# A two-stage mixture kernel: an in-place weight conversion with a leaky activation, a new plan for block 1's tokens and a reciprocal's correction factor in PSUM

## The chip, the cores and the metric

The kernel runs on one core of one Trainium2 chip. The metric is the time of one execution on the device in microseconds (us), the median of three runs. A core has TensorE (matmuls, PE in the rows; its weight loads are PEld), VectorE (DVE), ScalarE (ACT), GpSimd (POOL) and SyncE, whose queue (SP) issues all the DMAs here. Each engine works through its own instructions in order and waits on semaphores for the others.

## The reference

Attention with pooled keys and values, then two dense layers with a nonlinearity between, then a gated pair of them:

```python
k_p = k.reshape(B, H, Sp, 8, D).mean(axis=3)          # v_p likewise; B=8, H=8, S=576, D=64
scores = q @ k_p.T / sqrt(D)
x = softmax(scores) @ v_p                             # 4608 tokens x 512

h = x @ w_in                                          # 512 -> 2048
P = a[0] + a[1]*h + a[2]*h**2 + a[3]*h**3
Q = 1.0 + abs(b[0])*abs(h) + abs(b[1])*h**2
x = (P / (Q + 1e-6)) @ w_out                          # 2048 -> 512

gate = 1.0 / (1.0 + exp(-(x @ w_gate)))               # 512 -> 1536
out = (gate * (x @ w_val)) @ w_out2                   # 1536 -> 512
```

q, k, v are float32, the weights float64. The result has float32 accuracy, so each matmul operand is held as a high and a low part (hi and lo), and each product takes three matmuls (lines 485 to 487).

## The kernel before

**First stage.** The 4608 tokens are nine blocks of 512. For each block the hidden layer is walked in 16 steps of 128 columns, 144 steps n in all, `f = n % 16`. Step n multiplies block `n // 16` by weight slice f (`g1`, 12 matmuls, output h in PSUM), makes the rational function of h (`rational1` to `rational3`), splits the previous step's result into hi and lo (`split_g`) and multiplies step n - 3's result by its slice of w_out (`g2`, 12 matmuls, accumulated over the block in four banks acc). Four other PSUM banks rotate for everything else: h, and the scores, transposes and outputs of attention (sc, pta and ptb, psx).

**The rational function.** ScalarE makes s = h², u = |b0 h| and a linear y from h, VectorE makes u = Q - 1 and y towards P (lines 528 to 530). ScalarE writes a guess of 1/Q over h in PSUM, by way of Ln and Exp (`rational2`, line 538). `rational3` makes one correction step on VectorE: line 542 forms u = (u + 1) times the guess, line 543 y = P times the guess, line 544 y = (u - 2) times y. The bank of h comes free once its last reader is done, line 543.

**Attention beside it.** A block's tokens lie in four or five tiles (`token_tiles`). Tile i has a step `at[i]`; scores go on TensorE three steps ahead of it, exponential and normalisation (line 388 on GpSimd) two steps ahead. For tiles with `at[i] > NF1` ("late") the transposes stand in step `at[i]` behind g1 and the attention matmuls (`attend`, psx) in the step after, behind g1; for the others the transposes end step `at[i] - 1`, and `attend` stands in step `at[i]`. Block 1's five tiles have steps 3, 5, 7, 10, 12. `attend` writes xs, the block's input of g1. `on_pe` parts 0 and 1 of a step stand behind g1 and behind g2; `off_pe` parts 0, 1 and 2 hold the other engines' work. Keys and values of the next batch are pooled and masked by the same plan (`pool_k`, `pool_v`, `mask_v`).

**Weights.** They come as float64. A word pair is turned into a float32 pair in place: `conv1a` scales the high word's float view and the low word on ScalarE; `conv1b`, run by `gap()` between `rational2` and `rational3` of the next step, shifts the high word left by three into a work tile wx, puts its sign bit back by AND and OR (both VectorE), and adds the low word (GpSimd). `conv2` makes hi (ScalarE) and lo (GpSimd, line 118). In block 0 `weights_a` brings one slice of w_in and one of w_out through this per step: conv2 of w_in's slice n + 3 and w_out's n, conv1 of n + 5 and n + 2. From step 16 on `background` prepares the twelve units of the second stage's weights, eight steps each, 96 steps in all, and writes them to DRAM.

**Second stage.** From the end of step 143 on (`gate`, `value`, `h2`), it works on 768 tokens at a time in six rounds. The change doesn't touch it.

Line 542 to 544, in full:

```python
nc.vector.scalar_tensor_tensor(out=u, in0=u, scalar=ONE, in1=r, op0=ALU.add, op1=ALU.mult)
nc.vector.scalar_tensor_tensor(out=y, in0=y, scalar=coef[:, 0:1], in1=r, op0=ALU.add, op1=ALU.mult)
nc.vector.scalar_tensor_tensor(out=y, in0=u, scalar=-2.0, in1=y, op0=ALU.add, op1=ALU.mult)
```

## Time and profile before

| what | us |
|---|---|
| timed runs, median (lowest to highest) | 1896.74 (1896.67 to 1898.65) |
| profiled execution | 1894.58 |
| its span, first to last instruction | 1892.7 |
| prologue, to the first activation of step 0 | 44.6 |
| block 0 (steps 0 to 15) | 157.9 |
| blocks 1 to 6 | 657.3 |
| block 7 | 100.2 |
| block 8 and the second stage | 932.7 |

A block is counted from the first activation on its first h (line 525) to that of the next block. Busy time of an engine is the time in which it had an instruction under way; a TensorE that is busy all the time need not be at its peak, since each matmul's end is modelled. PEclk is the granted share of TensorE's full clock. A wait row says who waited, for whom, how long in total, how often, and the longest. A line number is that of kernel.py before.

### The profile page before, as it was taken

How to read it: one execution, taken by the hardware profiler on the slowest of the kernel's cores; microseconds unless marked ns; L12 is line 12 of the kernel's file. 1: busy time of each engine (PE TensorE's matmuls, PEld its weight loads, DVE VectorE, ACT ScalarE, POOL GpSimd, SP SyncE). 2: the span in 40 equal slices, each digit the busy share in tenths (PEclk: the TensorE clock that was granted, in tenths of full speed). 3: DMA queues.
4: the chain of work that ended last, by engine and by line, in shares of the span. 5: the costliest groups of instructions: out<-in, count | busy, mean ns of one | idle time of the engine just before them, and what ended most of it. 6: DMA issues, size and time to landing. Idle time of an engine off the chain costs nothing.

```text
span 1892.7 us, 25138 instructions
## 1 busy us (share of the span) xinstructions
PE 1804.6 (95%) x8936; PEld 1564.4 (83%) x8936; DVE 1242.5 (66%) x1847; ACT 943.0 (50%) x1754; POOL 896.4 (47%) x855
## 2 busy tenths in 40 slices
PE   5578999999999999999999999999999999999999
PEld 4467788787777788788887999998998998998997
DVE  7999999999998899988778543343334333333331
ACT  4777777677676777776666422222222222222221
POOL 6768556565564665653224234334235225235231
PEclk9799999999999999999999999999999999999999
DMA  7343355343544553443154574574573664663661
GB/s 247 131 153 120 107 191 187 135 171 135 186 159 156 192 176 137 168 148 119 56 196 150 190 236 153 166 235 133 184 228 123 211 211 129 222 201 112 206 203 43
DMA packets 123117, 312.56 MB, mean 165 GB/s; under 512 B 11504, under 2 KB 43248, under 8 KB 122992
## 3 DMA queue, kind: packets, MB, share of 16 engines
q1 hardware_dynamic: 122992, 310.95, 48.7%
q8 instruction: 71, 1.16, 0.2%
q14 instruction: 54, 0.44, 0.1%
HBM read 257.95 MB, written 52.95 MB: 164 GB/s over the span
## 4 chain that ended last, share of the span: by engine, by line
PE 67%; DVE 21%; ACT 4%; issue 4%; DMA 2%; POOL 2%; SPq 0%; ACTq 0%; POOLq 0%; DVEq 0%
PE h L485 13%; PE h L487 12%; PE h L486 12%; PE acc L485 3%; PE acc L487 3%; PE acc L486 3%; PE accA L722 3%; PE accA L723 3%; PE h L722 3%; PE h L723 3%; PE accA L721 3%; PE h L721 3%; DVE u L528 3%; PE psx L413 3%; DVE y L544 3%
## 5 line engine op out<-in xcount | busy, mean ns | idle before, releaser
L658 DVE TENSOR_TENSOR t<-h,t 128x384 f32<-128x384 f32 x360 | 200.7, 557 | 387.0 <-ACT t L666 276.2
L513 POOL TENSOR_TENSOR g<-y,g 128x512 fp32r<-128x512 f32 x144 | 190.6, 1324 | 245.7 <-ACT g L510 186.7
L711 POOL TENSOR_TENSOR t<-t 128x384 f32<-128x384 f32 x72 | 84.4, 1172 | 448.9 <-issue 253.7
L485 PE MATMUL h<-xs,wi 128*128 128x512 f32 x576 | 234.4, 407 | 11.8 <-DVE xs L420 5.2
L485 PE MATMUL acc<-g,wo 128*128 128x512 f32 x576 | 232.8, 404 | 2.2 <-ACT g L510 2.2
L487 PE MATMUL h<-xs,wi 128*128 128x512 f32 x576 | 229.3, 398 | 3.0 <-DVE xs L420 3.0
L486 PE MATMUL h<-xs,wi 128*128 128x512 f32 x576 | 229.2, 398 | 0.0
L487 PE MATMUL acc<-g,wo 128*128 128x512 f32 x576 | 226.0, 392 | 2.4 <-POOL g L513 2.4
L486 PE MATMUL acc<-g,wo 128*128 128x512 f32 x576 | 225.0, 391 | 0.0
L487 PE MATMUL h<-xS,wq 128*128 128x384 f32 x576 | 193.1, 335 | 0.0
L485 PE MATMUL h<-xS,wq 128*128 128x384 f32 x576 | 192.9, 335 | 0.0
L486 PE MATMUL h<-xS,wq 128*128 128x384 f32 x576 | 192.7, 335 | 0.0
L528 DVE SCALAR_TENSOR_TENSOR u<-s,coef,u 128x512 f32<-128x512 f32 x144 | 132.1, 918 | 32.2 <-ACT u L526 31.9
L485 PE MATMUL h<-xA,wq 128*128 128x384 f32 x432 | 149.0, 345 | 0.0
L544 DVE SCALAR_TENSOR_TENSOR y<-u,y 128x512 f32<-128x512 f32 x144 | 143.9, 999 | 4.9
L487 PE MATMUL h<-xA,wq 128*128 128x384 f32 x432 | 144.7, 335 | 0.0
L486 PE MATMUL h<-xA,wq 128*128 128x384 f32 x432 | 144.6, 335 | 0.0
L485 PEld LDWEIGHTS h<-xs,wi 128*128 128x128 f32 x576 | 111.3, 193 | 39.1 <-DVE xs L420 4.2
L525 ACT ACTIVATE s<-h 128x512 f32<-128x512 f32 x144 | 85.0, 590 | 110.4 <-PE h L487 110.3
L542 DVE SCALAR_TENSOR_TENSOR u<-u,h 128x512 f32<-128x512 f32 x144 | 98.5, 684 | 56.0 <-ACT h L538 54.3
L487 PEld LDWEIGHTS h<-xs,wi 128*128 128x128 f32 x576 | 111.1, 193 | 27.9 <-DVE xs L420 3.5
L485 PEld LDWEIGHTS acc<-g,wo 128*128 128x128 f32 x576 | 108.5, 188 | 27.9 <-ACT g L510 2.6
(122 smaller groups left out, 4300.2 us busy)
## 6 DMA issues: line engine op xcount, KB each, us to landing
wq<-w2d SPq DMA_DIRECT2D x252, 512.0 KB, 4.3
wo<-wod SPq DMA_DIRECT2D x88, 512.0 KB, 3.8
w2d<-wq SPq DMA_DIRECT2D x36, 512.0 KB, 2.9
x2d<-o SPq DMA_DIRECT2D x36, 256.0 KB, 2.4
out_dram<-o SPq DMA_DIRECT2D x36, 256.0 KB, 2.0
raw<-in_k_dram SPq DMA_DIRECT2D x32, 256.0 KB, 2.8
raw<-in_q_dram SPq DMA_DIRECT2D x32, 256.0 KB, 2.7
raw<-in_v_dram SPq DMA_DIRECT2D x32, 256.0 KB, 3.1
```

The source lines that it names most:

```text
L485: nc.tensor.matmul(out_, wl, xh, start=start, stop=False, skip_group_check=on)
L486: nc.tensor.matmul(out_, wh, xh, start=False, stop=False, skip_group_check=on)
L487: nc.tensor.matmul(out_, wh, xl, start=False, stop=stop, skip_group_check=on)
L513: eng.tensor_tensor(out=g[:, 1], in0=y, in1=g[:, 0].bitcast(F32), op=ALU.subtract)
L525: nc.scalar.activation(s, h, AF.Square)
L528: nc.vector.scalar_tensor_tensor(out=u, in0=s, scalar=coef[:, 5:6], in1=u, op0=ALU.mult, op1=ALU.add)
L542: nc.vector.scalar_tensor_tensor(out=u, in0=u, scalar=ONE, in1=r, op0=ALU.add, op1=ALU.mult)
L544: nc.vector.scalar_tensor_tensor(out=y, in0=u, scalar=-2.0, in1=y, op0=ALU.add, op1=ALU.mult)
L658: nc.vector.tensor_tensor(out=out_, in0=a, in1=b, op=ALU.add)
L721: nc.tensor.matmul(a[t], gh, wt[:, 0], start=(f == 0), stop=False)
L722: nc.tensor.matmul(a[t], gh, wt[:, 1], start=False, stop=False)
L723: nc.tensor.matmul(a[t], gl, wt[:, 0], start=False, stop=(f == NF2 - 1))
```

## The change

Six edits. In the conversion the Copy on the high word becomes a Prelu with the slope 2^32 on negative values: positive values are scaled by 2^-112 and negative ones by 2^-80, and the bits of the exponent in which these differ are such that the shift by three puts the sign bit where it belongs. The AND/OR instruction and the work tile wx go, and the shift writes in place. lo of w_in's slices is made on VectorE. Background's twelve units are spread over 112 steps (9 or 10 each, the last ones idle). Block 1's tiles get steps 2, 5, 8, 11, 14 and the late order (`late_` for every `at[i] > 0`), and pooled values and masks follow. `rational3` takes y first, writes the correction factor over the guess in PSUM, and multiplies from there. Of a block's four stores three and not two are copied by ScalarE.

```diff
-            nc.scalar.activation(hw.bitcast(F32), hw.bitcast(F32), AF.Copy, scale=2.0 ** -112)
+            nc.scalar.activation(hw.bitcast(F32), hw.bitcast(F32), AF.Prelu, scale=2.0 ** -112, alpha=2.0 ** 32)
...
-        ws = [(raw[:, :, 1], raw[:, :, 0], new_tmp("wx").bitcast(I32)[:, :raw.shape[1]]) for raw in raws]
-        for hw, lw, x in ws:
-            nc.vector.tensor_scalar(out=x, in0=hw, scalar1=3, scalar2=None, op0=ALU.logical_shift_left)
-        for hw, lw, x in ws:
-            nc.vector.scalar_tensor_tensor(out=hw, in0=hw, scalar=-2 ** 31, in1=x, op0=ALU.bitwise_and, op1=ALU.bitwise_or)
-        for hw, lw, x in ws:
+        ws = [(raw[:, :, 1], raw[:, :, 0]) for raw in raws]
+        for hw, lw in ws:
+            nc.vector.tensor_scalar(out=hw, in0=hw, scalar1=3, scalar2=None, op0=ALU.logical_shift_left)
+        for hw, lw in ws:
             nc.gpsimd.tensor_tensor(out=hw, in0=hw, in1=lw, op=ALU.add)
...
-        conv2(wi_raw.pop(f), wi[f][:, 0], wi[f][:, 1])
+        conv2(wi_raw.pop(f), wi[f][:, 0], wi[f][:, 1], nc.vector)
...
-        if not 0 <= n < 8 * NF2:
+        span = (NB - 2) * NF1
+        if not 0 <= n < span:
             return
-        u, r = divmod(n, 8)
+        u = n * NF2 // span
+        r = n + (-u * span // NF2)
...
-                at[i] = NF1 * (blk - 1) + SH[blk == 1] + m * (NF1 - (0, 1)[blk == 1] - SH[blk == 1]) // len(idx) if blk else m - len(idx)
+                at[i] = NF1 * (blk - 1) + (2 + 3 * m if blk == 1 else 1 + m * (NF1 - 1) // len(idx)) if blk else m - len(idx)
...
-            late_ = at[i] > NF1
+            late_ = at[i] > 0
...
-                st = e0 + c * (e1 - 3 - e0) // (2 * NCH)
+                st = e0 + c * (e1 - (3 if w == "k" else 1) - e0) // (2 * NCH)
...
-            put(e1 + (e1 > NF1), 1, 0, 0, ew, mask_v, b)
+            put(e1 + (e1 > 0), 1, 0, 0, ew, mask_v, b)
...
-            nc.vector.scalar_tensor_tensor(out=u, in0=u, scalar=ONE, in1=r, op0=ALU.add, op1=ALU.mult)
             nc.vector.scalar_tensor_tensor(out=y, in0=y, scalar=coef[:, 0:1], in1=r, op0=ALU.add, op1=ALU.mult)
-            nc.vector.scalar_tensor_tensor(out=y, in0=u, scalar=-2.0, in1=y, op0=ALU.add, op1=ALU.mult)
+            nc.vector.scalar_tensor_tensor(out=r, in0=u, scalar=ONE, in1=r, op0=ALU.add, op1=ALU.mult)
+            nc.vector.scalar_tensor_tensor(out=y, in0=r, scalar=-2.0, in1=y, op0=ALU.add, op1=ALU.mult)
...
-                    store(acc[i][e], x2d[i][:, e], e < 2, *(("su", 3) if e == NJ - 1 else ()))
+                    store(acc[i][e], x2d[i][:, e], e < 3, *(("su", 3) if e == NJ - 1 else ()))
```

Two places in the built order. The first is VectorE in step 1 of block 0, a step with two conversions. Before (wiraw and woraw are the float64 words of a w_in and a w_out slice, wx the work tile):

```order
L528 SCALAR_TENSOR_TENSOR u<-s,coef,u 128x512
L529 TENSOR_TENSOR y<-h,y 128x512
L530 SCALAR_TENSOR_TENSOR y<-y,coef,h 128x512
L98 TENSOR_SCALAR wx<-wiraw 128x512
L100 SCALAR_TENSOR_TENSOR wiraw<-wiraw,wx 128x512
L98 TENSOR_SCALAR wx<-woraw 128x512
L100 SCALAR_TENSOR_TENSOR woraw<-woraw,wx 128x512
L542 SCALAR_TENSOR_TENSOR u<-u,h 128x512
L543 SCALAR_TENSOR_TENSOR y<-y,coef,h 128x512
L544 SCALAR_TENSOR_TENSOR y<-u,y 128x512
```

The same step on VectorE in the changed program, whose line numbers are its own (h is the PSUM tile with the guess):

```order
L529 SCALAR_TENSOR_TENSOR u<-s,coef,u 128x512
L530 TENSOR_TENSOR y<-h,y 128x512
L531 SCALAR_TENSOR_TENSOR y<-y,coef,h 128x512
L100 TENSOR_SCALAR wiraw<-wiraw 128x512
L100 TENSOR_SCALAR woraw<-woraw 128x512
L543 SCALAR_TENSOR_TENSOR y<-y,coef,h 128x512
L544 SCALAR_TENSOR_TENSOR h<-u,h 128x512
L545 SCALAR_TENSOR_TENSOR y<-h,y 128x512
L118 TENSOR_TENSOR wi<-wiraw,wi 128x512
```

Two of ten instructions are gone, one has come in at the end, and the last product reads h and no longer u.

The second place is TensorE around the transposes of block 1's third tile, in step 6 of block 0 before (with buffer numbers; e is the normalised scores):

```order
L485 MATMUL acc3_741<-g_795,wo_762 128x512
L486 MATMUL acc3_741<-g_795,wo_762 128x512
L487 MATMUL acc3_741<-g_795,wo_762 128x512
L395 MATMUL pta_1003<-ident_118,e_842 128x128 x4
L396 MATMUL ptb_1004<-ident_118,e_842 64x128
L485 MATMUL h_1028<-xs_319,wi_847 128x512
```

In the changed program, in step 8:

```order
L488 MATMUL h_1044<-xs_317,wi_884 128x512
L397 MATMUL pta_1057<-ident_118,e_879 128x128 x4
L398 MATMUL ptb_1058<-ident_118,e_879 64x128
L486 MATMUL acc0_712<-g_933,wo_887 128x512
L487 MATMUL acc0_712<-g_933,wo_887 128x512
```

The transposes have moved from the end of a step, behind g2, to behind g1 of a later step, with g2 following.

## Rows read from the trace of the kernel before

**Rows 1.** Page, parts 1 and 2: busy us (share); tenths in 40 slices:

```profile
PE 1804.6 (95%) x8936; PEld 1564.4 (83%) x8936; DVE 1242.5 (66%) x1847; ACT 943.0 (50%) x1754; POOL 896.4 (47%) x855
PE   5578999999999999999999999999999999999999
...
DVE  7999999999998899988778543343334333333331
```

**Rows 2.** Windows: stretch, length; PE, PEld, DVE, ACT, POOL busy (count); PEclk; DMA:

```profile
44.64:202.53 157.89, 118.21 (x514) 95.23 (x515) 152.88 (x195) 112.19 (x199) 116.54 (x106) 0.87 0.38 131
...
307.70:422.33 114.63, 111.38 (x539) 91.06 (x538) 105.07 (x157) 79.01 (x149) 65.19 (x70) 0.99 0.45 159
...
859.79:959.97 100.18, 100.09 (x486) 83.37 (x485) 77.82 (x126) 63.76 (x114) 28.65 (x22) 1.00 0.26 89
```

**Rows 3.** Waits of TensorE, 48 to 206 us: total us, times, longest:

```profile
PE pta L395 <- POOL e L388: 31.1, 6, 12.1
PE h L485 <- DVE y L543: 2.6, 2, 2.3
PE psx L413 <- DVE y L543: 2.5, 3, 1.1
```

**Rows 4.** VectorE's groups, 48 to 206 us: count, busy us, mean ns, idle before:

```profile
L544 DVE SCALAR_TENSOR_TENSOR y<-u,y 128x512 f32<-128x512 f32 x16 | 23.6, 1474 | 0.6
L100 DVE SCALAR_TENSOR_TENSOR woraw<-woraw,wx 128x512 int32<-128x512 int32 x14 | 19.6, 1401 | 0.5
L98 DVE TENSOR_SCALAR wx<-wiraw 128x512 int32<-128x512 int32 x11 | 15.6, 1415 | 0.0
...
L100 DVE SCALAR_TENSOR_TENSOR wiraw<-wiraw,wx 128x512 int32<-128x512 int32 x11 | 11.9, 1084 | 0.4
L543 DVE SCALAR_TENSOR_TENSOR y<-y,coef,h 128x512 f32<-128x512 f32 x16 | 11.8, 736 | 0.0
L98 DVE TENSOR_SCALAR wx<-woraw 128x512 int32<-128x512 int32 x14 | 11.7, 835 | 0.0
```

**Rows 5.** ScalarE's groups, 48 to 206 us:

```profile
L92 ACT ACTIVATE woraw<-woraw 128x512 int32<-128x512 uint32 x14 | 9.4, 672 | 0.0
```

**Rows 6.** GpSimd's groups, 48 to 206 us:

```profile
L118 POOL TENSOR_TENSOR wi<-wiraw,wi 128x512 fp32r<-128x512 f32 x14 | 18.2, 1299 | 0.0
```

**Rows 7.** Single lines over the whole trace: ns minimum/median/maximum, first and last start:

```profile
L98 DVE TENSOR_SCALAR wx<-wqraw x36: 417/1245/1546, 224.7 to 856.1; 128x512 int32<-128x512 int32 x36
...
L100 DVE SCALAR_TENSOR_TENSOR wqraw<-wqraw,wx x36: 692/694/1112, 226.0 to 857.4; 128x512 int32<-128x512 int32 x36
...
L543 DVE SCALAR_TENSOR_TENSOR y<-y,coef,h x144: 733/740/745, 49.3 to 1055.1; 128x512 f32<-128x512 f32 x144
...
L544 DVE SCALAR_TENSOR_TENSOR y<-u,y x144: 691/693/6252, 50.1 to 1055.9; 128x512 f32<-128x512 f32 x144
```

**Rows 8.** Waits of TensorE, 206 to 860 us:

```profile
PE psx L413 <- DVE y L543: 5.2, 7, 1.1
PE pta L395 <- POOL e L388: 4.2, 5, 1.2
...
PE sc L358 <- DVE y L543: 1.8, 2, 1.3
...
PE h L485 <- DVE y L543: 0.4, 1, 0.4
```

**Rows 9.** Timeline in block 7: start us, us, engine, line, instruction:

```profile
888.91 0.74 DVE L543 SCALAR_TENSOR_TENSOR y<-y,coef,h 128x512 f32<-128x512 f32 x1
...
889.68 0.69 DVE L544 SCALAR_TENSOR_TENSOR y<-u,y 128x512 f32<-128x512 f32 x1
...
889.97 1.28 PE L413 MATMUL psx<-aT,vm 128*128 128x128 f32 x10
```

**Rows 10.** Waits of TensorE, 960 to 1060 us:

```profile
PE acc L487 <- POOL g L513: 2.4, 2, 2.0
PE acc L485 <- ACT g L510: 2.2, 1, 2.2
```

More of the change, by code (lines that the diff above doesn't have):

```diff
@@ L430, in attention_moe_glu_kernel @@
         of_block, first, last = {}, {}, {}
-        SH = (1, 3)
         for i, (b, t0, n) in enumerate(tiles):
```

## The prediction

> **What bounds the kernel now.** I read the page first, for the slices in which TensorE is not fully busy, then the windows by block, then who TensorE waits for in those windows, and last the groups of instructions on the engine that it waits for. The page shows TensorE at 95% of the span, with a weak stretch in the first slices, where VectorE is the full one [rows 1]. The windows make that exact: in block 0 (the 16 steps between 44.64 and 202.53 us) VectorE is busy for 152.9 of 157.9 us, while TensorE has 118.2 busy us, some of them at a granted clock of 0.87 [rows 2]. Block 7, which has the same matmuls and no weight conversion, takes 100.2 us. So some 58 us more than that lie in block 0, and the engine that is never idle there is VectorE. The waits agree: of TensorE's waits in this stretch 31.1 us are for GpSimd's normalised scores (tile e), 12.1 us of them once, and 5.1 us for a PSUM bank that VectorE's line 543 gives back [rows 3]. GpSimd's product is late because VectorE's sums ahead of it are late. After block 0 the picture is milder: block 2 takes 114.6 us with VectorE busy for 105.1, and VectorE is the fullest engine behind TensorE in all of blocks 1 to 6 [rows 2]. From 1057 us on no edit changes anything that matters; I take that part as unchanged.
>
> **The change part by part.** All sums are made against the profiled execution, 1894.58 us with its span of 1892.7; the median of the timed runs is 2.2 us above it.
>
> Conversion. The AND/OR instruction of line 100 goes. In the window of block 0 it ran 14 + 11 times at 1.401 and 1.084 us, 31.5 us of VectorE time [rows 4]. The shift of line 98 stays, but writes in place, to every second word. It costs 27.3 us in the same window for 25 [rows 4]; alone it takes 0.417, at worst 1.546 in the later conversions [rows 7]. Whether the strided write makes it slower no row tells: line 100, which writes the same words, takes 0.692 at best [rows 7], so the bounds are 25 x 0.42 = 10.5 and, with 0.28 more for the ones that run unhindered (about 10), 27.3 + 2.8 = 30 us. I take 27, nearest to its own rows. The scaling activation becomes a Prelu. The trace has no Prelu; the other activation of the conversion takes 0.672 [rows 5], and I take the same; the built order has no table load more than before.
>
> Correction factor. Line 542 wrote SBUF and will write PSUM; line 544 read two SBUF tiles and will read one PSUM and one SBUF tile, as line 543 does. In block 0 line 544 took 1.474 us on average and line 543 0.736 [rows 4]. Over the whole trace line 543 never leaves 0.733 to 0.745, while line 544 spreads from 0.691 to 6.252 [rows 7]: with two SBUF inputs it is held up, with one it is not. So 16 x (1.474 - 0.736) = 11.8 us go. No VectorE row writes PSUM; I take line 542's price for it, with 0 to 1 us more as the bound from line 543's. In an unhindered step the new form costs 0.05 us more. [...]
>
> Moved subtraction. Line 118 for the input weights goes from GpSimd to VectorE, 13 times in block 0. On GpSimd it takes 1.299 us [rows 6], so GpSimd loses 17 us, which lie beside other work. On VectorE it has two SBUF inputs, like line 544: 0.691 at best and 1.474 in block 0 [rows 4, 7]. With fewer GpSimd instructions to meet I take 1.1, so +14.3 us (bounds 9 to 19). It stands at the end of a step, behind ScalarE's copy; queued behind it is the next step's first VectorE instruction. The weights it makes are wanted three steps later, so TensorE doesn't feel it. [...]
>
> Block 0 as a sum: -31.5 - 11.8 + 14.3 = -29.0 us of VectorE work, out of 152.9. That leaves 124, about 118 of TensorE, and 112.2 of ScalarE [rows 2]. With three engines that near to each other VectorE will not be 97% busy any more. I add 5 us of idle time as now and 4 us for steps in which it waits for ScalarE, and get 133, **25 us less** (12 to 36: the dear ends of shift and subtraction with 8 us more idle time, or TensorE's own time).
>
> Plan of block 1's tokens. The five tiles move from steps 3, 5, 7, 10, 12 to 2, 5, 8, 11, 14; the transposes go behind the first product of that step, and the attention matmuls to the step after. Between normalisation and transposes lies now one more first product than before (3 us at most, half of block 7's 100.2 over 16 steps [rows 2]). That takes the sting out of the waits of 31.1 us [rows 3], but while VectorE is the bound the time lost is VectorE's work and not the place of the wait, so I book nothing on top. The last tile now lands in step 15, right ahead of block 1; later blocks end one step earlier. It hides behind the 12 matmuls of g2, as long as a first product; when VectorE lags more than that, a wait of 1 to 3 us appears there, and is in the range. The first scores go ahead of the first product: up to 2 us in the prologue against five AND/OR instructions saved there. I book 0 (-3 to +2).
>
> Blocks 1 to 6. The background conversion loses the AND/OR (36 times, 0.69 at best [rows 7]) and is spread over 112 steps and not 96; line 544 loses its long ones. But the bank with the guess is now given back by the last product, 0.74 us later. The place: in a step with transposes and no scores TensorE asks for the bank of the step's own first product. In block 7 psx starts at 889.97, 0.32 us after line 543 ended at 889.65; with the release at the end of the last product, 890.42, it waits 0.45 [rows 9]. In blocks 1 to 6 such waits already hold 5.2 + 1.8 us of the 20 that TensorE waits there, the other large one being 4.2 for e [rows 8]. What is within reach in these blocks is the 20 us (the sum of eight rows, of which four stand), and a few more that the clock loses after waits. I take 10 back from shorter lag and give 5 for 27 tiles x 0.2 us of bank wait: **-5** (-18 to +10).
>
> Block 7 was free of background work and now has 16 of 112 steps of it: **+3** (0 to +6). Block 8: TensorE waits 4.6 us for g, 2.4 of them for GpSimd [rows 10]; background ends two steps ahead of it and line 544 is no longer held: **-3** (-5 to +1). One store more per block goes to ScalarE, which has room.
>
> Sum: 0 - 25 - 5 + 3 - 3 = -30, so 1864.6 in the profile and **1866 us** for the median.
>
> **The rivals.** First, ScalarE takes VectorE's place in block 0. Between a step's exponential and the next step's first VectorE instruction it has six conversions and two more activations, eight at about 0.67 [rows 5] or 5.4 us, while VectorE then has only about 3.3 us to do (three of line 543's kind and the subtraction). If nothing else fills the 2 us gap, 13 steps have 26 us of new idle time: block 0 gives 8 us, and the whole -13, **1884**. For it: ScalarE's 112.2 us. Against it: attention's VectorE work falls into these gaps, and ScalarE was busy for only 71% of block 0.
>
> Second, on the slower side: the PSUM banks. Four serve both the first products and attention. All 40 tiles take a bank twice behind the last product (once for scores, once for psx); if every one waits the full 0.74 us longer, 80 x 0.74 = 59 us. It decides from about 47 such waits on, when they eat the 35 us won without them (25 + 10 - 3 + 3). All 80 would give 1896.7 - 35 + 59 = **1921**. For it: the waits of [rows 3, 8] on line 543 are this wait. Against it: their number is 15 or so, and the lag behind which the bank comes free shrinks with the work removed.
>
> Third, contention falls with the work: shift and first product (line 528) are held up by GpSimd less, block 0 goes to TensorE's bound and blocks 1 to 6 give 18: -36 - 18 + 3 - 4 = -55, **1842**.
>
> **How the numbers follow.** A difference under 0.2% (4 us) can't be told from none. My forecast has 0.74, with 1848 to 1881; ScalarE as next bound 0.13; the banks 0.05; less contention 0.08. The range reaches to 1886 at the upper end, to take in most of the ScalarE case, and stops at 1848. Faster: the forecast, the third case and most of the first, 0.91; same 0.04, the rest of the first; slower 0.05.
>
> **What would show it.** Right, if block 0 takes 122 to 146 us with VectorE still over 88% busy; if the last product of the rational shows 0.73 to 0.75 in every step; if the shift stays near 1 us and the moved subtraction near 1.1; and if TensorE's waits for e fall below 12 us in block 0. Wrong, if VectorE idles 20 us or more there with ScalarE as releaser (the first rival), or if waits for the last product at psx and sc grow past 20 us in blocks 1 to 7 (the second).

## The result and the profile after

The changed kernel takes **1846.96 us** (median of four runs, 1845.78 to 1847.87) against 1896.70 beside it: 0.9738 of the time before, interval 0.9721 to 0.9755, or 50 us less. The forecast was 1866 us with a range from 1848 to 1886. The direction is as forecast, and most of the gain lies where it was forecast; its size is not: it lies one microsecond outside the range.

By stretches of the two profiled executions (spans, us):

| stretch | before | after | difference | forecast |
|---|---|---|---|---|
| prologue | 44.64 | 40.68 | -4.0 | 0 |
| block 0 | 157.89 | 129.69 | -28.2 | -25 |
| blocks 1 to 6 | 657.26 | 644.84 | -12.4 | -5 |
| block 7 | 100.18 | 101.57 | +1.4 | +3 |
| block 8, to the end of the first activation on its last h | 90.19 | 84.31 | -5.9 | -3 |
| the rest | 842.54 | 843.32 | +0.8 | 0 |
| sum | 1892.7 | 1844.4 | -48.3 | -30 |

The page after, parts 1 and 2, to be laid beside [rows 1]: busy us and share of each engine, then tenths in 40 slices.

```profile
PE 1788.9 (97%) x8936; PEld 1556.9 (84%) x8936; DVE 1144.7 (62%) x1786; ACT 943.9 (51%) x1763; POOL 849.4 (46%) x839
...
PE   6689999999999999999999999999999999999999
...
DVE  6999887888788888888777343343343343343341
```

VectorE has lost 97.8 us of busy time over the whole program, and TensorE's weak start has shrunk from four slices to three. The windows, in the columns of [rows 2]: prologue, block 0, blocks 1 to 6, block 7 and block 8.

```profile
0.00:40.68 40.68, 25.38 (x137) 21.77 (x138) 27.68 (x57) 19.90 (x41) 22.51 (x39) 1.00 0.84 283
40.68:170.36 129.68, 105.66 (x494) 85.23 (x493) 122.04 (x181) 109.71 (x199) 97.02 (x97) 0.92 0.47 161
...
170.36:815.20 644.84, 633.79 (x3088) 522.95 (x3087) 536.68 (x851) 459.65 (x852) 346.71 (x379) 1.00 0.45 156
815.20:916.77 101.57, 101.57 (x493) 84.68 (x492) 83.38 (x132) 76.84 (x142) 53.15 (x50) 1.00 0.38 135
...
916.77:1001.08 84.31, 82.94 (x366) 68.34 (x365) 67.79 (x95) 60.46 (x102) 33.77 (x22) 1.00 0.57 206
```

In block 0 VectorE is busy for 122.0 us where it was 152.9, which is 94% of the shorter stretch: it is still the fullest engine there. The prologue, and blocks 1 to 6 before, which the rows ahead don't show:

```profile
0.00:44.64 44.64, 25.36 (x129) 21.04 (x130) 32.34 (x57) 19.87 (x40) 27.32 (x46) 0.93 0.76 262
...
202.53:859.79 657.26, 636.50 (x3084) 521.53 (x3083) 597.45 (x902) 469.65 (x876) 393.79 (x407) 1.00 0.46 162
```

TensorE's waits after the change, 44 to 174 us, against [rows 3] (who waited for whom, total, times, longest):

```profile
PE pta L397 <- POOL e L390: 7.5, 1, 7.5
PE sc L360 <- ACT aT L401: 7.3, 5, 2.0
PE sc L360 <- DVE y L545: 3.5, 2, 3.1
...
PE psx L415 <- DVE y L545: 2.8, 3, 1.2
```

The wait for e has gone from 31.1 us in six to 7.5 in one. New are waits of the scores for ScalarE's copies of the transposes and for a bank, by the last product, line 545.

VectorE's groups, 44 to 174 us, against [rows 4] (count, busy us, mean ns, idle before):

```profile
L529 DVE SCALAR_TENSOR_TENSOR u<-s,coef,u 128x512 f32<-128x512 f32 x16 | 21.2, 1323 | 4.4 <-ACT u L527 4.3
...
L118 DVE TENSOR_TENSOR wi<-wiraw,wi 128x512 fp32r<-128x512 f32 x13 | 11.8, 909 | 0.0
L545 DVE SCALAR_TENSOR_TENSOR y<-h,y 128x512 f32<-128x512 f32 x16 | 11.1, 691 | 0.5
L544 DVE SCALAR_TENSOR_TENSOR h<-u,h 128x512 f32<-128x512 f32 x16 | 11.0, 685 | 0.0
L100 DVE TENSOR_SCALAR wiraw<-wiraw 128x512 int32<-128x512 int32 x11 | 10.9, 993 | 0.0
...
L100 DVE TENSOR_SCALAR woraw<-woraw 128x512 int32<-128x512 int32 x14 | 10.4, 744 | 0.0
```

Single lines over the whole trace (ns minimum/median/maximum):

```profile
L545 DVE SCALAR_TENSOR_TENSOR y<-h,y x144: 690/691/693, 46.2 to 1006.8; 128x512 f32<-128x512 f32 x144
...
L529 DVE SCALAR_TENSOR_TENSOR u<-s,coef,u x144: 698/751/4142, 41.9 to 1002.6; 128x512 f32<-128x512 f32 x144
...
L100 DVE TENSOR_SCALAR wqraw<-wqraw x36: 416/970/1903, 194.7 to 909.2; 128x512 int32<-128x512 int32 x36
...
L92 ACT ACTIVATE wqraw<-wqraw x36: 656/668/709, 189.1 to 902.4; 128x512 f32<-128x512 f32 x36
```

The last product, now with its factor in PSUM, takes 690 to 693 ns in all 144 steps, where it had ranged to 6252 [rows 7]. The hold-ups haven't left the engine, though. The first sum, u (line 528 before, 529 now), is the one instruction of the rational function that still reads two SBUF tiles; it has gone from a mean of 835 to 1323 ns in block 0 and reaches 4142. Its group before (48 to 206 us):

```profile
L528 DVE SCALAR_TENSOR_TENSOR u<-s,coef,u 128x512 f32<-128x512 f32 x16 | 13.4, 835 | 0.0
```

What holds it up shows in the timeline of the longest case (start us, us; first GpSimd's normalisation, then the sum):

```profile
76.26 1.49 POOL L390 TENSOR_TENSOR e<-e,r 64x576 f32<-64x576 f32 x1 [2.02 <-DVE r L389]
```

```profile
76.66 4.14 DVE L529 SCALAR_TENSOR_TENSOR u<-s,coef,u 128x512 f32<-128x512 f32 x1
```

The sum ends at 80.80, 0.55 us after the third GpSimd instruction in a row (80.25). In four steps of this block 0 the normalisation begins 0.4 to 0.5 us ahead of the sum, and the sum takes 1.5 to 4.1 us; in the kernel before it begins 0.05 to 0.23 us behind the sum in five steps, and the sum takes 0.69 to 0.75 us. In the three other long ones a subtraction of GpSimd (line 118) had begun first.

### The profile page after: what moved, and what is told of

It reads as the page before. It is cut to its first block, busy times and chain, and to the rows that moved or that the text cites. A ratio compares the mean times of both kernels' runs of the same rounds, so it can differ in the third digit from the quotient of the medians.

```text
span 1844.4 us, 25043 instructions
## 1 busy us (share of the span) xinstructions
PE 1788.9 (97%) x8936; PEld 1556.9 (84%) x8936; DVE 1144.7 (62%) x1786; ACT 943.9 (51%) x1763; POOL 849.4 (46%) x839
## 4 chain that ended last, share of the span: by engine, by line
PE 75%; DVE 8%; POOL 6%; ACT 4%; issue 4%; DMA 2%; SPq 0%; POOLq 0%; ACTq 0%
PE h L486 14%; PE h L488 14%; PE h L487 14%; PE acc L486 5%; PE acc L488 4%; PE acc L487 4%; PE psx L415 3%; PE accA L723 3%; PE accA L724 3%; PE h L723 3%; PE h L724 3%; PE accA L722 3%; PE h L722 3%; DVE u L529 1%; DVE y L531 1%
## 5 line engine op out<-in xcount | busy, mean ns | idle before, releaser
L486 PE MATMUL h<-xs,wi 128*128 128x512 f32 x576 | 230.7, 400 | 3.4 <-DVE y L545 1.9
L488 PE MATMUL h<-xs,wi 128*128 128x512 f32 x576 | 226.2, 393 | 0.3 <-DVE xs L422 0.3
L487 PE MATMUL h<-xs,wi 128*128 128x512 f32 x576 | 225.9, 392 | 0.0
L529 DVE SCALAR_TENSOR_TENSOR u<-s,coef,u 128x512 f32<-128x512 f32 x144 | 135.9, 944 | 67.4 <-ACT u L527 67.0
L543 DVE SCALAR_TENSOR_TENSOR y<-y,coef,h 128x512 f32<-128x512 f32 x144 | 107.2, 744 | 68.9 <-ACT h L539 67.6
L486 PEld LDWEIGHTS h<-xs,wi 128*128 128x128 f32 x576 | 109.1, 189 | 28.1 <-DVE y L545 2.8
L488 PEld LDWEIGHTS acc<-g,wo 128*128 128x128 f32 x576 | 108.1, 188 | 25.8 <-POOL g L514 1.8
L488 PEld LDWEIGHTS h<-xs,wi 128*128 128x128 f32 x576 | 109.1, 189 | 24.4 <-DVE xs L422 0.7
L486 PEld LDWEIGHTS acc<-g,wo 128*128 128x128 f32 x576 | 108.1, 188 | 24.8
```

The costliest lines, as they stand in the source:

```text
L486: nc.tensor.matmul(out_, wl, xh, start=start, stop=False, skip_group_check=on)
L487: nc.tensor.matmul(out_, wh, xh, start=False, stop=False, skip_group_check=on)
L488: nc.tensor.matmul(out_, wh, xl, start=False, stop=stop, skip_group_check=on)
L529: nc.vector.scalar_tensor_tensor(out=u, in0=s, scalar=coef[:, 5:6], in1=u, op0=ALU.mult, op1=ALU.add)
```

## The experiments

The theory to be tested: block 0's gain comes from VectorE's work, nearly all of it from the conversion and the last product, and the remaining 18 us that the forecast lacked are the same two edits in other places. The rivals: that the plan of block 1's tokens, booked at nothing, brings part of it, and that the later release of the bank costs nothing or, against that, eats a gain which would else be larger. Each "undo" takes one edit out of the changed kernel, each "only" puts edits into the kernel before; r_hold, v_early and u_psum are variants of the changed kernel. All times, with the ratio to the kernel before on the same chip (interval), and the stretches of each profile:

| kernel | median | ratio | prologue | block 0 | VectorE in it | blocks 1 to 6 | block 8 |
|---|---|---|---|---|---|---|---|
| before | 1896.7 | 1 | 44.6 | 157.9 | 152.9 | 657.3 | 90.2 |
| changed | 1847.0 | 0.9738 (0.9721 to 0.9755) | 40.7 | 129.7 | 122.0 | 644.8 | 84.3 |
| c_undo | 1878.0 | 0.9902 (0.9887 to 0.9916) | 45.0 | 147.9 | 142.7 | 652.4 | 84.3 |
| c_only | 1866.3 | 0.9840 (0.9824 to 0.9857) | 39.7 | 142.8 | 126.4 | 647.9 | 90.5 |
| r_undo | 1853.9 | 0.9773 (0.9756 to 0.9789) | 40.2 | 132.9 | 128.1 | 644.0 | 89.9 |
| r_only | 1881.4 | 0.9923 (0.9908 to 0.9938) | 45.0 | 153.0 | 143.8 | 653.3 | 84.8 |
| r_hold | 1863.9 | 0.9828 (0.9813 to 0.9843) | 41.2 | 134.4 | 127.9 | 650.4 | 90.7 |
| s_undo | 1845.1 | 0.9728 (0.9714 to 0.9743) | 39.7 | 130.9 | 116.9 | 643.7 | 84.3 |
| p_undo | 1849.7 | 0.9751 (0.9737 to 0.9766) | 40.7 | 134.3 | 116.9 | 642.6 | 84.3 |
| cr_only | 1858.8 | 0.9800 (0.9786 to 0.9815) | 39.1 | 141.7 | 116.2 | 646.0 | 88.2 |
| v_early | 1849.3 | 0.9749 (0.9735 to 0.9764) | 43.7 | 130.2 | 121.4 | 642.4 | 87.1 |
| b_undo | 1846.9 | 0.9732 (0.9716 to 0.9748) | 40.9 | 129.6 | 122.0 | 644.6 | 87.7 |
| st_undo | 1846.3 | 0.9734 (0.9719 to 0.9748) | 40.1 | 128.4 | 120.8 | 644.2 | 84.8 |
| u_psum | 1832.1 | 0.9657 (0.9642 to 0.9671) | 40.5 | 121.6 | 110.3 | 638.0 | 85.0 |

The intervals are about 3 us to each side, so differences of 2 or 3 us between two medians tell nothing. A stretch in a single profile differs by 1 us between kernels that don't differ there, block 8 by up to 3.4 (b_undo).

### The conversion: c_undo and c_only

c_undo is the changed kernel with the old conversion; c_only is the kernel before with the new one, the reverse of this edit.

```diff
-            nc.scalar.activation(hw.bitcast(F32), hw.bitcast(F32), AF.Prelu, scale=2.0 ** -112, alpha=2.0 ** 32)
+            nc.scalar.activation(hw.bitcast(F32), hw.bitcast(F32), AF.Copy, scale=2.0 ** -112)
...
+            nc.vector.scalar_tensor_tensor(out=hw, in0=hw, scalar=-2 ** 31, in1=x, op0=ALU.bitwise_and, op1=ALU.bitwise_or)
```

> The changed kernel with the old conversion (Copy, shift to wx, AND/OR), all else as changed. Theory 1, VectorE's work: 25 AND/OR at 0.8 to 1.4 us return to block 0, block 0 20 to 28 us longer, prologue 4 longer since the AND/OR stands ahead of the last xs again, blocks 1 to 6 some 6 longer; about 1880. Rival, the plan carries the gain: block 0 under 8 us longer, total under 1858.

> The kernel before with the new conversion alone (Prelu, shift in place, no AND/OR). Theory, VectorE's work: block 0 loses 31 us of VectorE time, prologue 3 to 4 us, blocks 1 to 6 some 6; 1897 becomes about 1862. Rival, without the plan the waits for e hold: under 15 us gain, 1882 or more.

Measured: 31 us lost without it, 31 us won by it alone (1866.31 against 1897.15 beside it), near to the 1880 and 1862 expected. In block 0 it gave less than expected: c_only takes 26.5 us off VectorE there and 15.1 off the time. It is the largest edit by far, and it works in three places: 15 to 18 us in block 0, 8 to 9 us in blocks 1 to 6, and 4 to 5 us in the prologue, where the forecast had booked nothing net. The windows of c_undo, prologue and block 0:

```profile
0.00:44.98 44.98, 26.98 (x137) 22.90 (x138) 33.35 (x64) 20.01 (x40) 24.59 (x42) 0.96 0.82 283
44.98:192.87 147.89, 111.27 (x494) 89.91 (x493) 142.67 (x207) 110.47 (x200) 95.14 (x94) 0.88 0.40 133
```

VectorE has 20.6 us more to do than in the changed kernel (142.7 against 122.0), and block 0 is 18.2 us longer. Why the prologue gains is in the waits. Before, TensorE stood for VectorE's last part of the first block's input, in the middle of the very first product (waits, 0 to 48 us):

```profile
PE h L487 <- DVE xs L420: 3.0, 1, 3.0
```

and VectorE's timeline before shows what stood ahead of that subtraction:

```profile
36.40 0.41 DVE L98 TENSOR_SCALAR wx<-wiraw 128x512 int32<-128x512 int32 x1
36.84 0.69 DVE L100 SCALAR_TENSOR_TENSOR wiraw<-wiraw,wx 128x512 int32<-128x512 int32 x1
37.45 0.42 DVE L98 TENSOR_SCALAR wx<-woraw 128x512 int32<-128x512 int32 x1
37.91 1.41 DVE L100 SCALAR_TENSOR_TENSOR woraw<-woraw,wx 128x512 int32<-128x512 int32 x1
39.24 0.68 DVE L420 TENSOR_TENSOR xs<-psx,xs 128x512 fp32r<-128x512 f32 x1
```

Four instructions of the conversion, 2.9 us. After the change two shifts of 0.42 us stand there and the subtraction starts at 37.34, with a wait of 0.3 us left. The product behind it also ran at a lower clock before: the prologue's granted clock is 0.93 before and 1.00 after. Before, in the last 4.64 us of the prologue (40.00 to 44.64), with TensorE busy throughout, it was 0.50, after TensorE had been busy for 0.73 us in the 4 us ahead (36.00 to 40.00); after the change it is 1.00 up to the prologue's end.

### The correction factor in PSUM: r_undo, r_only, r_hold

r_undo is the changed kernel with the old `rational3`; r_only is the kernel before with the new one, the reverse of this edit.

```diff
+            nc.vector.scalar_tensor_tensor(out=u, in0=u, scalar=ONE, in1=r, op0=ALU.add, op1=ALU.mult)
             nc.vector.scalar_tensor_tensor(out=y, in0=y, scalar=coef[:, 0:1], in1=r, op0=ALU.add, op1=ALU.mult)
-            nc.vector.scalar_tensor_tensor(out=r, in0=u, scalar=ONE, in1=r, op0=ALU.add, op1=ALU.mult)
-            nc.vector.scalar_tensor_tensor(out=y, in0=r, scalar=-2.0, in1=y, op0=ALU.add, op1=ALU.mult)
+            nc.vector.scalar_tensor_tensor(out=y, in0=u, scalar=-2.0, in1=y, op0=ALU.add, op1=ALU.mult)
```

> The changed kernel with the old rational3 (correction factor to SBUF, last product with two SBUF inputs), all else as changed. Theory 1, VectorE's work is what counts: the last product goes back to 1.2 to 1.5 us in block 0, block 0 gets 8 to 12 us longer, blocks 1 to 6 some 6, block 8 some 4; about 1866. Theory 2, the bank counts: the earlier release of the guess's bank gives back its 0.7 us per wait, waits for that bank at psx and sc vanish from blocks 0 to 7 (8 to 12 us), and the total stays within 4 us of 1847.

> The kernel before with the new rational3 alone. Theory, VectorE's work: 12 us less in block 0, some 6 in blocks 1 to 6 and 4 in block 8, about 1877. Rival, contention moves on: what the last product no longer waits, line 528 and the shift wait instead; 7 us in all as in the undo run, 1890.

Measured: 7 us lost without it, 16 us won by it alone (1881.45 against 1897.15 beside it). Neither theory gives the 1854 of r_undo by itself, and r_only lies between its two numbers. The held instruction is back in r_undo; its group in block 0 (42 to 172 us):

```profile
L545 DVE SCALAR_TENSOR_TENSOR y<-u,y 128x512 f32<-128x512 f32 x16 | 18.7, 1172 | 0.6
```

It costs VectorE 7.6 us more than the new form's 11.1 (the engine as a whole has 6.0 more), yet block 0 only 3.3. In blocks 1 to 6 nothing is lost, and block 8 gets 5.6 us longer. The windows of r_undo:

```profile
173.11:817.13 644.02, 633.03 (x3088) 521.55 (x3087) 555.00 (x851) 460.40 (x853) 360.42 (x379) 1.00 0.45 156
918.64:1008.53 89.89, 85.58 (x365) 69.46 (x364) 75.03 (x96) 61.27 (x102) 34.31 (x22) 0.96 0.54 193
```

The last product's hold-ups have not gone over to the sum u. Its groups in block 0 of r_undo (42 to 172 us) and of r_only (45 to 198 us):

```profile
L529 DVE SCALAR_TENSOR_TENSOR u<-s,coef,u 128x512 f32<-128x512 f32 x16 | 20.9, 1308 | 2.1 <-ACT u L527 2.0
```

```profile
L528 DVE SCALAR_TENSOR_TENSOR u<-s,coef,u 128x512 f32<-128x512 f32 x16 | 13.8, 865 | 6.1 <-ACT u L526 6.1
```

With the old last product, itself held up again, the sum is as dear as in the changed kernel (1323); with the new one alone it stays near the 835 of before. In r_only the shifts took up some of it: 32.0 us for 25 where they had 27.3 [rows 4]. The sum is dear with the new conversion alone (c_only, 1235 ns) and, with the old conversion, once plan and subtraction are new (c_undo, 1214). What of these puts it behind GpSimd's instructions was not separated.

Over all kernels block 8 lies between 84.3 and 88.2 us with the new order and between 89.9 and 90.7 without it. So that gain, too, belongs to this edit, though a part of it varies among the kernels that have it.

In blocks 1 to 6 VectorE is busy for 555.0 us in r_undo and 536.7 in the changed kernel, 18 us less for no time at all. Either these 18 us hide anyway, or the bank that is held longer takes them back. r_hold tells these apart: it has the old `rational3`, with its held product, and a copy of one column of the guess behind the product, which keeps the bank as long as the new order does, and somewhat longer.

```diff
             nc.vector.scalar_tensor_tensor(out=y, in0=u, scalar=-2.0, in1=y, op0=ALU.add, op1=ALU.mult)
+            nc.vector.tensor_copy(hold[:, 0:1], r[:, 0:1])
```

> The changed kernel with the old rational3 and, behind it, a VectorE copy of one column of the guess, so that the bank is held up to the end of the last product while nothing else of the old form changes (the copy costs VectorE some 0.1 us a step; its result is used by nobody). Against the run with the old rational3 alone (1854): if the bank's later release costs 0.7 us at 15 to 30 waits, 10 to 20 us longer, about 1868; if it lies in slack, under 5 us longer.

Measured: 10 us over r_undo, the low end of what was expected if the bank counts, 6.4 of them in blocks 1 to 6 (the copies alone are 0.15 us in each step). The waits of TensorE in 175 to 826 us:

```profile
PE psx L416 <- DVE hold L547: 8.3, 8, 1.9
PE h L487 <- DVE hold L547: 2.8, 3, 1.4
```

That is 11.1 us of waits for the bank. The same two rows are 1.3 us in r_undo (0.7 and 0.6), and in the changed kernel, 174 to 860 us:

```profile
PE sc L360 <- ACT aT L401: 4.1, 4, 1.7
PE psx L415 <- DVE y L545: 2.8, 4, 0.9
PE h L486 <- DVE y L545: 1.9, 2, 1.3
PE h L486 <- DVE xs L422: 1.4, 2, 1.0
PE pta L397 <- POOL e L390: 0.6, 1, 0.6
```

So the later release is not free: by itself it is worth at most 6 us in these blocks (VectorE's time for the copies is in that), and as r_undo and the changed kernel are equal there, the shorter last product gives about as much back.

### The moved subtraction and the plan: s_undo, p_undo, cr_only

s_undo leaves the lo part of w_in's slices on GpSimd; p_undo has the old plan (tiles in steps 3, 5, 7, 10, 12, with the transposes ahead).

```diff
-        conv2(wi_raw.pop(f), wi[f][:, 0], wi[f][:, 1], nc.vector)
+        conv2(wi_raw.pop(f), wi[f][:, 0], wi[f][:, 1])
```

> The changed kernel with the w_in subtraction back on GpSimd. Theory 1 in its plain form, VectorE's busy time: 11.8 us less for VectorE in block 0, block 0 5 to 10 us shorter, about 1840. Rival, contention: GpSimd has 17 us more and holds up the shift and line 529 for longer, and the normalisation waits behind it; block 0 equal or up to 6 us longer, 1847 to 1853.

```diff
-                at[i] = NF1 * (blk - 1) + (2 + 3 * m if blk == 1 else 1 + m * (NF1 - 1) // len(idx)) if blk else m - len(idx)
+                at[i] = NF1 * (blk - 1) + SH[blk == 1] + m * (NF1 - (0, 1)[blk == 1] - SH[blk == 1]) // len(idx) if blk else m - len(idx)
...
-            late_ = at[i] > 0
+            late_ = at[i] > NF1
```

> The changed kernel with the old plan (block 1's tiles at 3, 5, 7, 10, 12 and not late, values pooled earlier, masks as before). Theory 1: VectorE's work is the same, block 0 within 4 us, about 1849. Rival, the plan carries the gain: waits for e come back to 25 us and block 0 is 10 to 20 us longer, 1857 to 1867.

Both medians are within 3 us of the changed kernel's, which the intervals hardly tell apart. In block 0 p_undo is 4.6 us longer and s_undo 1.2. In p_undo TensorE's waits for e are 10.4 us (40 to 172 us) and not the 25 of the rival; s_undo's block 0 is as its rival had it. Both have VectorE at 116.9 us and not at 122.0, so neither stretch is set by VectorE's work alone. In s_undo the shift of w_in's words is dearer, with GpSimd busy for 112.2 us and not 97.0 (VectorE's groups, 40 to 171 us):

```profile
L100 DVE TENSOR_SCALAR wiraw<-wiraw 128x512 int32<-128x512 int32 x11 | 16.2, 1475 | 0.0
```

It takes 993 ns in the changed kernel, so 5.3 of the 11.8 us that the moved subtraction costs VectorE come back in this group alone.

By these two results plan and subtraction seem to be worth some 6 us together in block 0. cr_only asks that directly: the kernel before with new conversion and new `rational3`, and nothing else. The spread of the background work and the extra store don't touch block 0, so that what lacks there is plan and subtraction.

```diff
+            nc.scalar.activation(hw.bitcast(F32), hw.bitcast(F32), AF.Prelu, scale=2.0 ** -112, alpha=2.0 ** 32)
...
+            nc.vector.scalar_tensor_tensor(out=r, in0=u, scalar=ONE, in1=r, op0=ALU.add, op1=ALU.mult)
+            nc.vector.scalar_tensor_tensor(out=y, in0=r, scalar=-2.0, in1=y, op0=ALU.add, op1=ALU.mult)
```

> The kernel before with the new conversion and the new rational3, and nothing else. If these two carry the gain: alone they gave 31 and 16 us, undone 31 and 7, so together 38 to 47, 1850 to 1859. If plan, spread, subtraction and store are needed for them to work, over 1862.

Measured: 1858.8 us, 38 of the 50 us, at the dear end of the first expectation. Block 0 takes 141.7 us, 12.0 more than the changed kernel, not 6. Its window, then VectorE's largest wait and TensorE's waits there (39 to 181 us):

```profile
39.10:180.77 141.67, 114.27 (x521) 92.80 (x522) 116.18 (x169) 110.45 (x199) 110.54 (x109) 0.89 0.43 147
```

```profile
DVE u L528 <- ACT u L526: 22.2, 12, 5.3
```

```profile
PE sc L358 <- ACT aT L399: 11.5, 3, 4.9
PE pta L395 <- POOL e L388: 10.8, 3, 8.0
PE h L485 <- POOL wi L118: 4.4, 1, 4.4
```

Here VectorE is busy for only 82% of the stretch and waits 22.2 us for ScalarE's first activations, while TensorE waits 10.8 us for e and 11.5 for ScalarE's copies of the transposes. The stretch is no longer bound by VectorE's work: the engines wait for each other in turn. With the plan alone added (s_undo) 10.8 of the 12.0 us go, with the subtraction alone (p_undo) 7.4: either edit does most of the work of the other. How they do so was not taken apart further.

### The pooled values: v_early

One wait of 7.5 us for e is left in block 0 of the changed kernel. v_early lets the second batch's values be pooled one step earlier, as before.

```diff
-                st = e0 + c * (e1 - (3 if w == "k" else 1) - e0) // (2 * NCH)
+                st = e0 + c * (e1 - (3 if w == "k" or b == 1 else 1) - e0) // (2 * NCH)
```

> The changed kernel with the pooling of the second batch's values spread as before (ending one step earlier), so that GpSimd isn't busy with it when block 1's first scores are to be normalised. If that pooling makes TensorE's wait of 7.5 us for e in step 2, the wait falls to 3 to 4 us and the total to about 1843; if it is VectorE's lag, nothing changes.

Measured: 1849.3 us, no gain: the pooling makes little of the wait, which fell only from 7.5 to 6.1. That it is VectorE's lag isn't shown by this. The prologue is 3.0 us longer in this profile, where the scores wait 12.7 us for q's transfer; in the changed kernel they wait 2.9 for it and 7.6 for the pooled keys. In step 0 four additions of the conversion, right behind the pooled values, ran in a row on GpSimd beside VectorE's first sum (timeline, first VectorE, then the first and the last of GpSimd's four: start us, us):

```profile
44.87 3.46 DVE L529 SCALAR_TENSOR_TENSOR u<-s,coef,u 128x512 f32<-128x512 f32 x1 [2.60 <-ACT u L527]
```

```profile
43.75 1.03 POOL L102 TENSOR_TENSOR wiraw<-wiraw 128x512 int32<-128x512 int32 x1
...
46.74 1.03 POOL L102 TENSOR_TENSOR woraw<-woraw 128x512 int32<-128x512 int32 x1
```

The sum starts at 44.87 and ends at 48.33, about when the last of the four ends (47.77): an instruction of 0.70 us at best was held up for 2.8 us, by several GpSimd instructions one behind the other.

### Spread and stores: b_undo, st_undo

```diff
-        u = n * NF2 // span
-        r = n + (-u * span // NF2)
+        u, r = divmod(n, 8)
```

> The changed kernel with background's twelve units over 96 steps again, 8 each. If the thinner spread relieves blocks 1 to 6, they are 3 to 8 us longer and block 7 1 to 2 us shorter, about 1850. If VectorE has room there by now, the total stays within 2 us of 1847.

```diff
-                    store(acc[i][e], x2d[i][:, e], e < 3, *(("su", 3) if e == NJ - 1 else ()))
+                    store(acc[i][e], x2d[i][:, e], e < 2, *(("su", 3) if e == NJ - 1 else ()))
```

> The changed kernel with two of a block's four stores on ScalarE and two on VectorE, as before. Expected by every theory here: within 3 us of 1847, since 9 copies of 0.7 us change engines and neither engine is TensorE's bound at that place.

Measured: no difference from the changed kernel in either. In b_undo's profile block 7 is 1.0 us shorter and block 8 is 3.4 longer, which the medians (1846.93 and 1846.96) don't bear out as a gain or loss of the whole.

### The other two-input sum: u_psum

If what is left of the hold-ups sits on the one instruction that still reads two SBUF tiles, giving that one an operand from PSUM should free it. The sum |b0 h| + |b1| h² is the absolute value of (|b1 h| + |b0|) h, and h itself lies in PSUM. So ScalarE makes |b1 h|, VectorE adds |b0| and multiplies by h, and ScalarE takes the absolute value ahead of the logarithm, in the place of the square that is no longer needed: the count of instructions on each engine stays, and so does the function computed.

```diff
-            nc.scalar.activation(s, h, AF.Square)
-            nc.scalar.activation(u, h, AF.Abs, scale=coef[:, 4:5])
+            nc.scalar.activation(u, h, AF.Abs, scale=coef[:, 5:6])
...
-            nc.vector.scalar_tensor_tensor(out=u, in0=s, scalar=coef[:, 5:6], in1=u, op0=ALU.mult, op1=ALU.add)
+            nc.vector.scalar_tensor_tensor(out=u, in0=u, scalar=coef[:, 4:5], in1=h, op0=ALU.add, op1=ALU.mult)
...
+            nc.scalar.activation(u, u, AF.Abs)
```

> The changed kernel with u made another way: ScalarE gives |b1 h|, VectorE (|b1 h| + |b0|) times h with h read from PSUM, ScalarE takes the absolute value ahead of Ln; no square. The function is the same; no VectorE instruction of the rational function has two SBUF inputs any more, and ScalarE has as many instructions as before, but one of them now stands in the chain between u and the guess. If contention for SBUF is what the instruction for u pays (1.32 us on average in block 0, 0.75 unhindered), it falls to 0.75, block 0 loses 6 to 10 us and the total is about 1838. If the longer chain counts (0.6 us a step later release of the bank), blocks 1 to 6 lose as much as block 0 wins: 1845 to 1852.

Measured: **1832.07 us**, 15 us below the changed kernel and 0.9657 of the time before (0.9642 to 0.9671): the fastest kernel of this case. The sum's line over the whole trace, and the windows of block 0 and blocks 1 to 6:

```profile
L528 DVE SCALAR_TENSOR_TENSOR u<-u,coef,h x144: 689/747/751, 41.9 to 988.0; 128x512 f32<-128x512 f32 x144
```

```profile
40.48:162.10 121.62, 103.36 (x494) 83.80 (x493) 110.34 (x180) 112.21 (x199) 92.99 (x97) 0.94 0.50 171
162.10:800.07 637.97, 630.91 (x3088) 522.25 (x3087) 511.35 (x852) 474.38 (x852) 331.38 (x379) 1.00 0.45 158
```

No step holds it up any more (751 ns at most, 4142 before that edit). VectorE has 11.7 us less in block 0, which gets 8.1 us shorter, as expected, and 25.3 us less in blocks 1 to 6, which get 6.9 us shorter; that was not expected, and the total lies 6 us below the 1838. In block 0 ScalarE (112.2 us) has now passed VectorE (110.3) as the fullest engine.

## What the prediction had right, and which of its steps failed

The forecast's sum, 30 us less than 1896.7, makes 1866.7 and was put down as 1866. The profiles differ by 48.3 us where 30 were forecast. Of the 18.3 us between, 7.4 lie in blocks 1 to 6, 4.0 in the prologue, 3.2 in block 0, 2.9 in block 8 and 1.6 in block 7; the rest takes back 0.8. Two terms lie outside their own bounds, the prologue (-3 to +2) and block 8 (-5 to +1).

**The bound.** That block 0 was set by VectorE's work holds for the edits together. The engine lost 30.9 us there (forecast 29), and the stretch 28.2 (forecast 25); c_undo puts 20.6 us of work back and 18.2 us of time. Put into the kernel before one by one, the edits give back only some half of the work that they remove: c_only 15.1 us for 26.5, r_only 4.9 for 9.1. VectorE is 94% busy in the stretch, inside the announced condition of over 88%. Of the surplus of 3 us some 2 are work, the rest idle time: 9 us were forecast, 7.6 are left.

**The prices in block 0.** The last product was taken at line 543's 0.736 and takes 0.691 in every step; the announced sign of 0.73 to 0.75 is not there. Line 542 (0.676), which has a constant as scalar too, would have been the nearer row. The bound upwards for a write to PSUM, 0 to 1 us, wasn't needed: line 544, which writes there, takes 0.685 on average. In the quiet steps, too, the last product is no dearer with an operand in PSUM: 0.05 us more were forecast for each, and the trace shows 0.691 against 0.691 at best before. The shift was taken at 27 us for 25 and takes 21.3; in place and to every second word it still takes 0.416 at best. The moved subtraction was taken at 1.1 and measures 0.909, 13 times. Against these three gains of together 9 us stands the one that the forecast left where it was: the sum u, which rose from 835 to 1323 ns, 7.8 us. The last product's hold-ups, gone there, are not its cause: the sum is as dear in r_undo, and stays at 865 in r_only. That the two errors nearly cancel is luck.

**The prologue: a step that failed.** "I book 0 (-3 to +2)" set the first scores against the AND/OR instructions. The measured -4.0 us lies outside the bounds. The working priced the instructions and didn't look at what was queued behind them: the wait of 3.0 us for xs (line 420) was in the trace, with four conversion instructions right ahead of that line. c_undo has the old prologue (44.98), c_only the new one (39.66), r_only the old one (45.05), which leaves the conversion as the cause. How much of the 4.0 us is the wait (3.0 to 0.3) and how much the clock behind it was not separated.

**Blocks 1 to 6: a term that was mis-sized.** -5 was 10 back from the shorter lag and 5 paid for the bank; it became -12.4. The bank's side is about right: TensorE's waits for it are 4.7 us in the changed kernel against 1.3 with the old order, and r_hold shows that holding it costs time, 6.4 us there. The other side was too small: with 3.4 to 6.4 us for the bank, the shorter lag gave back some 16 to 19 us (an estimate, 12.4 and the bank's) and not 10. The conversion alone is worth 7.6 (c_undo) to 9.3 us (c_only) there, and the last product, once it is no longer held, has to be added: VectorE's 18 us less of it pay for the bank. The waits of 20 us in [rows 8], and a few more for the clock, were taken as what is within reach (the clock fell once there in the trace before: it was 0.64 from 360 to 364 us, behind 4 us with 1.27 us of TensorE work). The waits fell to 10.8, and TensorE's busy time fell as well, from 636.5 to 633.8, with a granted clock of 1.00 in both rows; why it fell isn't shown.

**Block 8** was forecast at -3 and gave -5.9, nearly all by the last product (r_undo 5.6). TensorE's wait for g there is one of 1.4 us where [rows 10] had 4.6, and the granted clock of the stretch rose from 0.98 to 1.00. With block 8 varying by some 3 us among kernels with the new order, how far it lies beyond its bounds is uncertain. **Block 7** gave +1.4 for +3, the second stage 0.8 for 0.

**The plan: a step whose reasoning failed.** It was booked at nothing "on top", since the time lost was VectorE's work and not the place of the wait. With less work that no longer holds: p_undo is 4.6 us longer in block 0, and without plan and subtraction (cr_only) it is 12 us, with VectorE idle for 25. There conversion and last product take 36.7 us of VectorE's work out of block 0 and only 16.2 of its time. The other 12.0 of the 28.2 us need the plan or the moved subtraction, and neither was booked for a gain; that 25 was forecast and 28.2 came is in part luck. The subtraction was booked at +14.3 us of VectorE work and takes 11.8. Without it (s_undo) VectorE has 5.1 us less to do and block 0 is 1.2 longer, so it cost no time; part of the reason is in the shifts of w_in's words, 1475 ns there against 993.

**The rivals.** ScalarE as the next bound is not what the changed kernel shows: 4.3 us of waits for its u in front of VectorE in block 0. Its sign, VectorE idle for 20 us and more with ScalarE as releaser, appears in cr_only, that is without plan and subtraction. The banks cost what the forecast had paid for them and not 59 us; the waits for the last product at psx and sc are 2.8 us in blocks 1 to 7, for which the sign of 20 was given, and 6.3 in block 0. The third rival, less contention at 1842, is the nearest to the result. Its mechanism is there in part only: the shift runs freer, the sum u does not. It had a chance of 0.08, and the range stopped six microseconds above it. The shift, the moved subtraction and the share of blocks 1 to 6 all came out at the cheap side. All three may hang on how often VectorE and GpSimd meet, and the range took such errors as if they were apart; that one cause moved them together is argued, not shown. That VectorE is held up beside GpSimd is in the trace before: all 62 last products (line 544) over 0.78 us and all 49 shifts (line 98) over 0.46 us begin while an instruction of GpSimd is under way, and 7 of the 82 and 5 of the 19 shorter ones do. Of the rational function's instructions those that read one operand from PSUM stay within 0.69 to 0.75 us (lines 543 and 545, and 528 in u_psum), and the one that reads two from SBUF goes to 4.1 us. A shift, which reads one tile, is held up too: 0.416 us at best, up to 1.903 in the later conversions.

## What to carry to other kernels

Where VectorE is the bound beside a busy GpSimd, list its instructions with two SBUF inputs, and those of one input that the trace shows held up, like the shifts here. Look for one operand of each that lies in PSUM or can be put there: both times that was tried the instruction was no longer held up in any step (at most 693 ns for the last product, 751 for the sum). See in the timeline which engine's instruction starts first; an edit elsewhere can put an instruction that was free behind a running one of GpSimd, as it did the sum u. Look in the queue of the bounding engine for what stands ahead of the one instruction that another engine waits for, in the prologue above all, and book that wait, not only the instructions. And edits that each measure next to nothing when undone alone can be worth much together, as plan and subtraction are here, 12 us of block 0: undo them together before calling them idle.

## What the runs showed of the hardware

A scalar_tensor_tensor of 128 x 512 with its first operand in PSUM and the second in SBUF (line 545) takes 0.691 us, the same as the best with two SBUF operands. With the PSUM tile as second operand it takes 0.685 in line 544, whose scalar is a constant, and 0.739 in line 543, whose scalar is a column of coef; which operand lies in PSUM does not explain the difference, and whether the column does was not tested. Writing the result to PSUM costs next to nothing: 0.685 us (line 544) against the 0.676 that the same instruction took in block 0 before, into SBUF. A shift of every second word in place keeps, at best, the 0.416 us that it had into a dense tile (0.417 [rows 7]). Prelu on ScalarE takes 0.668 us, as the other activation of the conversion did (0.672 in [rows 5]). And VectorE's hold-up by GpSimd isn't bounded by one GpSimd instruction: beside four in a row of 1.03 us one sum of 0.70 us at best took 3.46 (v_early), and beside three one took 4.14 (the changed kernel).
